# Turning attention probabilities with VectorE blocks and DMA in place of TensorE transposes

## The chip, the cores and the metric

The kernel runs on one core of one Trainium2 chip. Its time is the device time of one execution in microseconds; the median of the runs shown is what counts. Engines are named as in the profile: PE is TensorE (PEld its weight loads), DVE is VectorE, ACT is ScalarE, POOL is GpSimd, SP is SyncE, which issues the transfers.

## What is computed

Sparse attention, and then a gated MLP on its result:

```python
scores = q @ k.T / sqrt(64) - slope[h] * dist       # B=4, H=8, S=768, D=64
keep   = (key < 8) | ((0 <= q_pos - k_pos) & (q_pos - k_pos < 96))
a      = softmax(where(keep, scores, -1e9))
x      = (a @ v) laid out as [3072, 512]
out    = ((x @ w_a) * (x @ w_b)) @ w_out            # 512 -> 1536 -> 512, all float32
```

A block of 128 queries needs its own 128 keys, the 96 before them and 8 global ones: 232 columns, or 128 or 256 for the first two blocks of a batch.

## The kernel before

The 24 blocks of 128 queries (4 batches of 6) are cut into eight units of 4, 2, 3, 3, 3, 3, 3, 3 blocks. A unit's attention gives x for its 256 to 512 tokens, and its MoE (`moe`, L866) multiplies them by the weights, which are loaded once (`load_w`, L405, in units 0 and 1's time) and stay in SBUF. While PE does the MoE of unit u, the attention of unit u+1 goes on beside it. Float32 values are held as a high and a low part, and three products (high x high, low x high, high x low) give one exact enough product; this is why each MoE product shows three matmuls.

The MoE of a unit has 12 steps. A step makes two projections p of 12 matmuls each (L902) into two PSUM banks, p0 and p1, copies the first out (L387), multiplies it by the second (L941), makes the high and low part (hh at L387 or L389, hl at L397), and adds the product with w_out of the step before to acc (L920, 3 matmuls for each of the unit's blocks). After the twelfth step acc is copied out and stored (L973), three stores a unit.

The attention of units 2 to 7 (`attention`, L819) goes over four pairs of heads and, in each, over two heads and the unit's three blocks. For each head the raw q and k are loaded (`fetch`, L514, SP, two buffers) and split (`split`, L530); v is loaded once a pair (L522). For each block:

- scores into a bank psS (L844),
- softmax into a tile t of [128 queries, keys] (L583 DVE, L599 ACT, L614 and L621 DVE, normalisation at L631 ACT or L633 DVE), three buffers,
- `turn` (L648): a PE transpose for each chunk of 128 keys (L658) into a bank psT, and one copy to pf (L387 ACT or L389 DVE), so that the keys lie on partitions; pf has six buffers.

A block has one chunk when it is the first of its batch, otherwise two. After a pair's six blocks the values (`values`, L663) are multiplied: for every chunk and both heads a matmul with v as the stationary and pf as the moving operand (L675), 20 or 24 in a group, and the result is copied to x. Units 0 and 1 (`quad`, L687) do the same two heads at a time in another layout, also with `turn`.

No loop of the program sets the order. Every operation goes into a plan (`Schedule`) with a due time, an estimated cost for each engine that may do it, and the buffers that it reads and writes. The plan is played through once: each engine takes, in order of due time, the first operation that is ready and whose buffers are free; cheap choices (ACT or DVE for a copy) fall to whoever is free. The order found is written out as five fixed queues, which wait for each other by semaphores. A transfer counts in the plan as time on one engine "dma", and 2300 ns more until its data may be used. The operations of the first two units are tried in 400 random variants and the best kept. Attention is spread over 12 - SLACK steps of the unit before it:

```python
xs[u] = self.attention(u, t, t + (NF - SLACK) * steps[u - 1])
```

Of the kernel before, what the change touches and what calls it, by code (L numbers as in the profile page):

```python
# [13 lines left out]
F32 = mybir.dt.float32  # L14
F32R = mybir.dt.float32r
I32 = mybir.dt.int32
# [9 lines left out]
P = 128  # L26
# [8 lines left out]
PAIRED = 2  # L35
RAWS = 2
TBUFS = 3
PFBUFS = 6
MBUFS = 3

START = 52000
WLEAD = 6000
LOADLEAD = 8000
SPLITLEAD = 3000
SLACK = 1.5
BACKLOG = 1.0


# [112 lines left out]
        return self.tile[key]  # L161


class Op:
    def __init__(self, index, due, costs, emit, reads, writes, spare, port):
        self.index, self.due, self.costs, self.emit, self.spare = index, due, costs, emit, spare
# [28 lines left out]
class Schedule:  # L195
# [7 lines left out]
        self.tags = {}  # L203

    def buf(self, *args, **kw):
        b = Buf(*args, **kw)
        self.tags.setdefault(b.tag, []).append(b)
        return b

# [142 lines left out]
class Fast:  # L352
# [13 lines left out]
    def open(self):  # L366
# [2 lines left out]
        self.sp = ctx.enter_context(tc.tile_pool(name="s", bufs=1))  # L369
        self.ps = ctx.enter_context(tc.tile_pool(name="ps", bufs=1, space=PSUM))  # L370

    def sbuf(self, shape, dtype, tag, name, bufs=1):
        return self.plan.buf(self.sp, shape, dtype, tag, name, bufs=bufs)

# [30 lines left out]
    def load_w(self, f, due):  # L405


        nc, op = self.nc, self.plan.op
        for g in range(2):
            raw = self.plan.buf(self.wp, [P, 2 * WN], I32, f"w{f}_{g}", f"wr{f}_{g}")  # L410
            w = self.plan.buf(self.wp, [P, 2 * WN], F32R, f"w{f}_{g}", f"wt{f}_{g}")
            self.w[f, g] = w
            st = self.sbuf([P, WN], I32, "wm", f"wm{f}_{g}", MBUFS)
            words = lambda raw=raw: raw[:, :].rearrange("p (n two) -> p n two", two=2)
            low = lambda words=words: words()[:, :, 0]
            high = lambda words=words: words()[:, :, 1]
            mi = lambda st=st: st[:, :]
            m = lambda st=st: st[:, :].bitcast(F32)
            op(
                due,  # L420
                lambda e, f=f, g=g, raw=raw: nc.sync.dma_start(raw[:, :].bitcast(I64), self.wts[f, g]),
                writes=[(raw, "lo"), (raw, "hi")],
                dma=2184,
            )
            op(
                due,
                lambda e, m=m, high=high: nc.scalar.activation(m(), high().bitcast(F32), AF.Abs),  # L427
                [(raw, "hi")],
                [st],
                act=act(WN) + 72,  # L430
            )
            op(
                due,
                lambda e, m=m: nc.vector.tensor_scalar(
                    m(), m(), EMIN, EMAX, op0=ALU.max, op1=ALU.min
                ),
                [],
                [st],
                port=BOTH,
                dve=dve(WN, True),  # L440
            )
            op(
                due,
                lambda e, mi=mi: nc.vector.tensor_scalar(
                    mi(), mi(), 3, 0x3FFFFFFF, op0=ALU.logical_shift_left, op1=ALU.bitwise_and
                ),
                [],
                [st],
                port=BOTH,
                dve=dve(WN, True),  # L450
            )
            op(
                due,
                lambda e, mi=mi, high=high: nc.vector.scalar_tensor_tensor(
                    mi(), high(), -0x40000000, mi(), op0=ALU.bitwise_and, op1=ALU.bitwise_or
                ),
                [(raw, "hi")],
                [st],
                port=BOTH,
                dve=dve(WN),  # L460
            )
            op(
                due,
                lambda e, low=low: nc.scalar.activation(  # L464
                    low(), low().bitcast(U32), AF.Copy, scale=2.0**-29
                ),
                [],
                [(raw, "lo")],
                act=act(WN) + 72,
            )  # L470
            op(
                due,
                lambda e, mi=mi, low=low: nc.vector.tensor_tensor(mi(), mi(), low(), op=ALU.add),
                [(raw, "lo")],
                [st],
                port=BOTH,
                dve=dve(WN),
            )
            hi, lo = (lambda w=w: w[:, :WN]), (lambda w=w: w[:, WN:])
            self.copy(due, hi, m, WN, [st], [(w, "H")])  # L480
            self.sub(due, lo, m, hi, WN, [st, (w, "H")], [(w, "L")], shared=False)
# [91 lines left out]
            )  # L573
        return qh, ql, kk

    def softmax(self, h, due, wins, ps, t, sm):

        nc, op, n = self.nc, self.plan.op, len(wins)
        for j, (o, w) in enumerate(wins):
            neg = self.negd if w > P else self.negd0  # L580
            op(
                due,
                lambda e, j=j, o=o, w=w, neg=neg: nc.vector.tensor_tensor_reduce(  # L583
                    t[:, o : o + w],
                    ps[:, o : o + w],
                    neg[:, :w],
                    -(2.0 ** -(h + 1)),
                    3.0e38,
                    ALU.add,
                    ALU.min,  # L590
                    sm[:, j : j + 1],
                ),
                [ps, neg],
                [(t, j), (sm, j)],
                dve=dve(w) + 10,
            )
            op(
                due,
                lambda e, j=j, o=o, w=w: nc.scalar.activation(  # L599
                    t[:, o : o + w],  # L600
                    t[:, o : o + w],
                    AF.Exp,
                    bias=sm[:, j : j + 1],
                    scale=-1.0,
                    accum_out=sm[:, n + j : n + j + 1],
                ),
                [(sm, j)],
                [(t, j), (sm, n + j)],
                act=act(w) + 200,
            )  # L610
# [34 lines left out]
                act=act(w) + 100,  # L645
            )

    def turn(self, due, wins, t, pt, pf, spare=0.0):  # L648

        nc = self.nc  # L650
        starts = []
        for o, w in wins:
            starts += [o] if w == P else [o, o + w - P]
        n = len(starts) * P

        def emit(e):
            for c, o in enumerate(starts):
                nc.tensor.transpose(pt[:, c * P : c * P + P], t[:, o : o + P], self.ident)  # L658

        self.plan.op(due, emit, [t], [pt], pe=len(starts) * 112, spare=spare)  # L660
        self.copy(due, lambda: pf[:, :n], lambda: pt[:, :n], n, [pt], [pf], psum=True)

    def values(self, due, pl, blocks, v, probs, pa):  # L663


        nc = self.nc

        def emit(e):
            for i in blocks:
                slots = pl.vslot[i]  # L670
                for c, slot in enumerate(slots):
                    for s in range(2):
                        pf, o = probs[s, i]
                        v0 = (s * pl.nv + slot) * D
                        nc.tensor.matmul(  # L675
                            pa[D * s : D * s + D, i * P : i * P + P],
                            v[:, v0 : v0 + D],
                            pf[:, o + c * P : o + c * P + P],
                            start=c == 0,
                            stop=c == len(slots) - 1,  # L680
                        )

        reads = [v] + [probs[s, i][0] for s in range(2) for i in blocks]
        n = sum(len(pl.vslot[i]) for i in blocks)
        self.plan.op(due, emit, reads, [pa], pe=n * 218 + 290, spare=SPARE if pl.late else 0.0)

    def quad(self, u, c, j, due, raw, v, pa, homes):  # L687
# [44 lines left out]
        for s in range(2):  # L732
# [11 lines left out]
            self.turn(due, wins, t, pt, pf)  # L744
            o = 0
            for i in blocks:
                probs[s, i] = (pf, o)
                o += len(pl.vslot[i]) * P
        if pa is None:
            pa = self.bank("psS", f"pa{n}")  # L750
# [68 lines left out]
    def attention(self, u, start, end):  # L819
# [8 lines left out]
        for c in range(NCC):  # L828
            probs = {}
            v = self.fetch_v(u, c, start + (2 * c + 1) * step - LOADLEAD)  # L830
            for s in range(2):
                h = 2 * c + s
                due = start + h * step
# [2 lines left out]
                for i in range(pl.nb):  # L836
                    due = start + h * step + (i + 1) * step / pl.nb
                    k0, w = pl.kwin[i]
                    n = f"{u}_{h}_{i}"
                    ps = self.bank("psS", "ps" + n)  # L840

                    def scores(e, i=i, k0=k0, w=w, ps=ps, qh=qh, ql=ql, kk=kk):
                        for m, q in enumerate((qh, ql)):
# [6 lines left out]
                            )  # L850

                    op(due, scores, [qh, ql, kk], [ps], pe=2 * pe(w))
                    t = self.sbuf([P, 2 * P], F32, "t", "t" + n, TBUFS)
                    sm = self.sbuf([P, 8], F32, "sm", "sm" + n, 6)
                    self.softmax(h, due, [(0, w)], ps, t, sm)
                    pt = self.bank("psT", "pt" + n)
                    pf = self.sbuf([P, 2 * P], F32, "pf", "pf" + n, PFBUFS)
                    self.turn(due, [(0, w)], t, pt, pf, SPARE)
                    probs[s, i] = (pf, 0)
            due = start + (2 * c + 2) * step  # L860
            pa = self.bank("psA", f"pa{u}_{c}")
            self.values(due, pl, range(pl.nb), v, probs, pa)
            self.result(u, c, due, pa, x)
# [514 lines left out]
```

## Time and profile before

| what | us |
|---|---|
| median of 3 runs | 767.13 (767.0 to 768.37) |
| the profiled execution | 766.51 |
| its span in the trace | 764.7 |
| PE busy | 743.8 |
| ACT busy | 434.6 |
| DVE busy | 427.5 |
| POOL busy | 5.8 |

The span is the time between the first and the last recorded instruction; the profiled execution is 1.8 us longer than that. A share of busy time is an average over the stages. Matmuls are pipelined: a row with 0.39 us may start its successor after 0.23, so the pace is read from the starts. In rows of groups stand the line, the engine, the operation, what it writes and reads, the count, and then the busy time, the mean ns of one, and the idle time before them with what ended it.

### The profile page before, as it was taken

The numbers are of one execution on the slowest core, as the hardware profiler recorded it, in microseconds if no ns is written. First come the engines' busy times: TensorE is split into PE (matmuls) and PEld (weight loads), VectorE is DVE, ScalarE is ACT, GpSimd is POOL, SyncE is SP. The second block draws the span as 40 slices with busy tenths as digits, with TensorE's granted clock in tenths as the row PEclk, the third lists the DMA queues.
The fourth block names the chain that finished last, engine by engine and source line by source line (L and its number), as shares of the span: only waits on it lengthen the run. The fifth ranks groups of instructions, "written<-read, shape, count | busy, mean of one in ns | idle before, by whom it ended". The sixth has DMA issues, their size and how long they took to land.

```text
span 764.7 us, 12536 instructions
## 1 busy us (share of the span) xinstructions
PE 743.8 (97%) x4608; PEld 661.7 (87%) x4608; DVE 427.5 (56%) x1367; ACT 434.6 (57%) x1101; POOL 5.8 (1%) x25
## 2 busy tenths in 40 slices
PE   5789999999999999999999999999999999999996
PEld 4567778799999989999989999899989999989995
DVE  6999999755665555454445554444553645422111
ACT  7999756566665655555555655565554655441111
POOL 1000000000000000000000000000000000000000
PEclk9999999999999999999999999999999999999998
DMA  7896010132222111111212211111122111010001
GB/s 281 353 402 270 20 29 16 45 110 63 61 89 61 57 39 48 62 42 49 61 47 75 61 58 31 49 59 48 51 61 68 48 47 41 1 41 1 1 1 45
DMA packets 20085, 57.25 MB, mean 75 GB/s; under 512 B 2352, under 2 KB 2608, under 8 KB 20016
## 3 DMA queue, kind: packets, MB, share of 16 engines
q1 hardware_dynamic: 20016, 56.37, 22.2%
q8 instruction: 38, 0.62, 0.3%
q14 instruction: 31, 0.25, 0.1%
HBM read 50.07 MB, written 6.29 MB: 74 GB/s over the span
## 4 chain that ended last, share of the span: by engine, by line
PE 92%; ACT 4%; DVE 3%; issue 1%; DMA 0%; ACTq 0%
PE p L902 51%; PE acc L920 26%; PE pa L675 5%; PE pt L658 5%; PE ps L844 4%; PE ps L722 1%; ACT t L599 1%; DVE kk L397 1%; DVE t L583 1%; ACT wr L464 1%; ACT t L631 1%; ACT pf L387 1%; ACT wm L427 1%; DMA nv<-ns 0%; DVE ql L551 0%
## 5 line engine op out<-in xcount | busy, mean ns | idle before, releaser
L902 PE MATMUL p<-xh,wt 128*128 128x384 f32 (+2 forms) x1488 | 440.0, 344 | 0.6 <-ACT raw L387 0.5
L902 PEld LDWEIGHTS p<-xh,wt 128*128 128x128 f32 x1488 | 272.6, 188 | 14.4 <-issue 2.7
L902 PE MATMUL p<-xl,wt 128*128 128x384 f32 (+2 forms) x816 | 269.7, 341 | 1.2 <-ACT xl L387 0.9
L920 PE MATMUL acc<-wt,hh 128*128 128x512 f32 x576 | 208.1, 398 | 0.0
L902 PEld LDWEIGHTS p<-xl,wt 128*128 128x128 f32 x816 | 153.7, 189 | 10.5 <-ACT xl L387 1.2
L920 PEld LDWEIGHTS acc<-wt,hh 128*128 128x128 f32 x576 | 108.2, 188 | 19.5 <-issue 0.9
L599 ACT ACTIVATE t<-t,sm 128x232 f32<-128x232 f32 (+2 forms) x192 | 91.5, 479 | 44.7 <-DVE sm L583 42.4
L920 PE MATMUL acc<-wt,hl 128*128 128x512 f32 x288 | 113.1, 393 | 0.0
L583 DVE CUSTOM_DVE_ANT_0 t<-ps,rel 128x232 f32<-128x232 f32 (+1 forms) x160 | 63.1, 401 | 86.5 <-PE ps L844 84.7
L941 DVE TENSOR_TENSOR raw<-p,raw 128x384 f32<-128x384 f32 (+2 forms) x96 | 53.3, 555 | 100.7 <-PE p L902 85.0
L631 ACT ACTIVATE t<-t,sm 128x232 f32<-128x232 f32 (+2 forms) x129 | 61.7, 482 | 54.3 <-DVE sm L621 52.8
L387 ACT COPY raw<-p 128x384 f32<-128x384 f32 (+2 forms) x95 | 45.6, 480 | 82.0 <-PE p L902 81.9
L387 ACT COPY pf<-pt 128x256 f32<-128x256 f32 (+3 forms) x153 | 56.8, 376 | 24.9 <-PE pt L658 23.5
L658 PE MATMUL pt<-ident,t 128*128 128x128 f32 x352 | 67.3, 278 | 3.4 <-DVE t L633 2.0
L397 DVE TENSOR_TENSOR hl<-raw,hh 128x384 fp32r<-128x384 f32 (+2 forms) x96 | 53.3, 556 | 24.4 <-ACT hh L387 24.0
L387 ACT CAST hh<-raw 128x384 fp32r<-128x384 f32 (+2 forms) x91 | 46.5, 511 | 28.6 <-DVE raw L941 28.4
L658 PEld LDWEIGHTS pt<-ident,t 128*128 128x128 f32 x352 | 44.2, 140 | 19.4 <-ACT t L631 7.5
L920 PEld LDWEIGHTS acc<-wt,hl 128*128 128x128 f32 x288 | 54.3, 188 | 6.7
L614 DVE TENSOR_SCALAR sm<-sm 128x1 f32<-128x1 f32 (+1 forms) x168 | 25.7, 153 | 39.2 <-ACT t L599 37.5
L675 PE MATMUL pa<-pf,v 128*64 128x128 f32 x640 | 42.4, 278 | 3.0 <-DVE xl L781 2.5
L675 PEld LDWEIGHTS pa<-pf,v 128*64 128x64 f32 x640 | 34.5, 136 | 11.9 <-issue 4.6
L397 DVE TENSOR_TENSOR kk<-raw,kk 64x348 fp32r<-64x348 f32 (+1 forms) x92 | 42.7, 464 | 2.9
(79 smaller groups left out, 599.2 us busy)
## 6 DMA issues: line engine op xcount, KB each, us to landing
wr<-wts SPq DMA_DIRECT2D x24, 768.0 KB, 12.7
raw<-qkv SPq DMA_DIRECT2D x24, 366.0 KB, 3.0
raw<-qkv SPq DMA_DIRECT2D x24, 314.0 KB, 2.9
v<-qkv SPq DMA_DIRECT2D x16, 384.0 KB, 3.1
out<-o SPq DMA_DIRECT2D x23, 256.0 KB, 2.0
v<-qkv SPq DMA_DIRECT2D x16, 256.0 KB, 2.6
raw<-qkv SPq DMA_DIRECT2D x3, 616.0 KB, 6.2
raw<-qkv SPq DMA_DIRECT2D x5, 360.0 KB, 3.9
```

What stands on the lines that cost most here:

```text
L387: self.nc.scalar.copy(out(), src())
L397: lambda e: self.engine(e).tensor_sub(out(), a(), b()),
L583: lambda e, j=j, o=o, w=w, neg=neg: nc.vector.tensor_tensor_reduce(t[:, o : o + w], ps[:, o : o + w], neg[:, :w], -(2.0 ** -(h + 1)), 3.0e ...
L599: lambda e, j=j, o=o, w=w: nc.scalar.activation(t[:, o : o + w], t[:, o : o + w], AF.Exp, bias=sm[:, j : j + 1], scale=-1.0, accum_out=sm[ ...
L614: lambda e: nc.vector.tensor_scalar_add(sm[:, 2 * n : 3 * n], sm[:, n : 2 * n], 1e-9),
L631: nc.scalar.mul(t[:, o : o + w], t[:, o : o + w], r)
L658: nc.tensor.transpose(pt[:, c * P : c * P + P], t[:, o : o + P], self.ident)
L675: nc.tensor.matmul(pa[D * s : D * s + D, i * P : i * P + P], v[:, v0 : v0 + D], pf[:, o + c * P : o + c * P + P], start=c == 0, stop=c == ...
L844: nc.tensor.matmul(ps[:, :w], q[:, i * P : i * P + P], kk[:, k0 : k0 + w], start=m == 0, stop=m == 1,)
L902: nc.tensor.matmul(p[:, :T], wt(), b[:, b0 : b0 + T], start=c == 0 and n == 0, stop=c == NCC - 1 and n == 2,)
L920: nc.tensor.matmul(acc[i][:, :], hs[:, i * P : i * P + P], wt(), start=f == 0 and n == 0, stop=f == NF - 1 and n == 2,)
L941: lambda e, asb=asb, pb=pb: nc.vector.tensor_mul(asb[:, :T], pb[:, :T], asb[:, :T]),
```

## The change

In units 2 to 7 the PE transposes and the copies out of psT go. In their place `blocks32` (DVE) transposes a block's t in squares of 32x32, within each group of 32 partitions, into a buffer tp of 12 chunks for the whole pair of heads; then `swap` issues 16 transfers (SP), each from one group of 32 partitions of tp to one of pf, which carry the squares to the partitions of their keys. tp and pf are single buffers for a pair. The values read pf in four runs of 32 columns. tp, and three further buffers for t, lie in the scratch of the weight preparation (wm), which is idle by then; softmax in these units is made to wait for the last of it. The scores alternate between the banks psS and psT, and SLACK grows from 1.5 to 3. Units 0 and 1 keep `turn`.

```diff
-PFBUFS = 6
+CHUNKS = 12
+SQ = 32
-SLACK = 1.5
+SLACK = 3.0
...
+        self.wm = self.sbuf([P, MBUFS * WN], I32, "wm", "wm")
+        self.tp = self.plan.add(Over(self.wm, 0, CHUNKS * P, "tp"))
+        ats = range(CHUNKS * P, MBUFS * WN, 2 * P)
+        self.spares = [self.plan.add(Over(self.wm, at, 2 * P, f"t{at}")) for at in ats]
...
+    def blocks32(self, due, w, t, slot, n):
+        nc, tp = self.nc, self.tp
+        def emit(e):
+            src = t[:, :w]
+            dims = [[w - P, n]] * (n > 1) + [[SQ, P // SQ], [1, SQ]]
+            src = bass.AP(src.tensor, src.offset, [list(src.ap[0])] + dims)
+            dst = tp[:, :].rearrange("p (b m i) -> p m b i", b=P // SQ, m=CHUNKS)
+            dst = dst[:, slot : slot + n] if n > 1 else dst[:, slot]
+            nc.vector.transpose(dst, src)
+        done = [(self.wm, k) for k in range(MBUFS)]
+        self.plan.op(due, emit, [t] + done, [(tp, slot)], port=BOTH, dve=120 + 1.042 * n * P)
+
+    def swap(self, due, pf, m):
+        nc, tp, n = self.nc, self.tp, CHUNKS * SQ
+        for a in range(P // SQ):
+            for b in range(P // SQ):
+                out = lambda a=a, b=b: pf[SQ * b : SQ * b + SQ, a * n : a * n + m * SQ]
+                src = lambda a=a, b=b: tp[SQ * a : SQ * a + SQ, b * n : b * n + m * SQ]
+                self.plan.op(
+                    due,
+                    lambda e, out=out, src=src: nc.sync.dma_start(out(), src()),
+                    [tp],
+                    [(pf, (a, b))],
+                    dma=480,
+                )
...
             v = self.fetch_v(u, c, start + (2 * c + 1) * step - LOADLEAD)
+            pf = self.sbuf([P, CHUNKS * P], F32, "pf", f"pf{u}_{c}", 1)
+            slot = 0
...
-                    ps = self.bank("psS", "ps" + n)
+                    ps = self.bank(("psS", "psT")[(pl.nb * h + i) % 2], "ps" + n)
...
-                    t = self.sbuf([P, 2 * P], F32, "t", "t" + n, TBUFS)
+                    turn = (pl.nb * h + i) % (TBUFS + len(self.spares))
+                    if turn < TBUFS:
+                        t = self.sbuf([P, 2 * P], F32, "t", "t" + n, TBUFS)
+                    else:
+                        t = self.spares[turn - TBUFS]
...
-                    pt = self.bank("psT", "pt" + n)
-                    pf = self.sbuf([P, 2 * P], F32, "pf", "pf" + n, PFBUFS)
-                    self.turn(due, [(0, w)], t, pt, pf, SPARE)
-                    probs[s, i] = (pf, 0)
+                    chunks = len(pl.vslot[i])
+                    self.blocks32(due, w, t, slot, chunks)
+                    def get(k, slot=slot, pf=pf):
+                        view = pf[:, :].rearrange("p (a m i) -> p m a i", a=P // SQ, m=CHUNKS)
+                        return view[:, slot + k]
+                    probs[s, i] = (pf, get)
+                    slot += chunks
             due = start + (2 * c + 2) * step
+            self.swap(due, pf, slot)
```

More of the change, by code (lines that the diff above doesn't have):

```diff
@@ L161, in __getitem__, with __init__ @@
         return self.tile[key]
+class Over(Buf):
+    def __init__(self, home, at, cols, name):
+        super().__init__(None, None, F32, name, name)
+        self.home, self.at, self.cols = home, at, cols
+    def __getitem__(self, key):
+        if self.tile is None:
+            self.tile = self.home[:, self.at : self.at + self.cols].bitcast(F32)
+        return self.tile[key]
 class Op:
@@ L205, in buf, with add @@
     def buf(self, *args, **kw):
-        b = Buf(*args, **kw)
+        return self.add(Buf(*args, **kw))
+    def add(self, b):
         self.tags.setdefault(b.tag, []).append(b)
@@ L412, in load_w @@
             self.w[f, g] = w
-            st = self.sbuf([P, WN], I32, "wm", f"wm{f}_{g}", MBUFS)
+            ring = (2 * f + g) % MBUFS
+            st = (self.wm, ring)
+            m0 = ring * WN
             words = lambda raw=raw: raw[:, :].rearrange("p (n two) -> p n two", two=2)
@@ L416, in load_w @@
             high = lambda words=words: words()[:, :, 1]
-            mi = lambda st=st: st[:, :]
-            m = lambda st=st: st[:, :].bitcast(F32)
+            mi = lambda m0=m0: self.wm[:, m0 : m0 + WN]
+            m = lambda mi=mi: mi().bitcast(F32)
             op(
@@ L574, in split, with softmax @@
         return qh, ql, kk
-    def softmax(self, h, due, wins, ps, t, sm):
+    def softmax(self, h, due, wins, ps, t, sm, done=()):
         nc, op, n = self.nc, self.plan.op, len(wins)
@@ L592, in softmax @@
                 ),
-                [ps, neg],
+                [ps, neg, *done],
                 [(t, j), (sm, j)],
@@ L646, in softmax, with turn @@
             )
-    def turn(self, due, wins, t, pt, pf, spare=0.0):
+    def turn(self, due, wins, t, pt, pf):
         nc = self.nc
@@ L658, in emit @@
                 nc.tensor.transpose(pt[:, c * P : c * P + P], t[:, o : o + P], self.ident)
-        self.plan.op(due, emit, [t], [pt], pe=len(starts) * 112, spare=spare)
+        self.plan.op(due, emit, [t], [pt], pe=len(starts) * 112)
         self.copy(due, lambda: pf[:, :n], lambda: pt[:, :n], n, [pt], [pf], psum=True)
+    def blocks32(self, due, w, t, slot, n):
[22 more added lines that the diff above has]
+                )
     def values(self, due, pl, blocks, v, probs, pa):
@@ L672, in emit @@
                     for s in range(2):
-                        pf, o = probs[s, i]
                         v0 = (s * pl.nv + slot) * D
@@ L677, in emit @@
                             v[:, v0 : v0 + D],
-                            pf[:, o + c * P : o + c * P + P],
+                            probs[s, i][1](c),
                             start=c == 0,
@@ L746, in quad @@
             for i in blocks:
-                probs[s, i] = (pf, o)
+                get = lambda c, pf=pf, o=o: pf[:, o + c * P : o + c * P + P]
+                probs[s, i] = (pf, get)
                 o += len(pl.vslot[i]) * P
@@ L852, in attention @@
                     op(due, scores, [qh, ql, kk], [ps], pe=2 * pe(w))
-                    t = self.sbuf([P, 2 * P], F32, "t", "t" + n, TBUFS)
-                    sm = self.sbuf([P, 8], F32, "sm", "sm" + n, 6)
-                    self.softmax(h, due, [(0, w)], ps, t, sm)
-                    pt = self.bank("psT", "pt" + n)
-                    pf = self.sbuf([P, 2 * P], F32, "pf", "pf" + n, PFBUFS)
-                    self.turn(due, [(0, w)], t, pt, pf, SPARE)
-                    probs[s, i] = (pf, 0)
+                    turn = (pl.nb * h + i) % (TBUFS + len(self.spares))
[3 more added lines that the diff above has]
+                        t = self.spares[turn - TBUFS]
+                    sm = self.sbuf([P, 8], F32, "sm", "sm" + n, 6)
+                    self.softmax(h, due, [(0, w)], ps, t, sm, [(self.wm, k) for k in range(MBUFS)])
+                    chunks = len(pl.vslot[i])
[3 more added lines that the diff above has]
+                        return view[:, slot + k]
+                    probs[s, i] = (pf, get)
+                    slot += chunks
             due = start + (2 * c + 2) * step
+            self.swap(due, pf, slot)
             pa = self.bank("psA", f"pa{u}_{c}")
```

## The prediction

> **What bounds the kernel now.** I read the page first: busy time, the 40 slices, the chain that ended last.
>
> ```profile
> span 764.7 us, 12536 instructions
> PE 743.8 (97%) x4608; PEld 661.7 (87%) x4608; DVE 427.5 (56%) x1367; ACT 434.6 (57%) x1101; POOL 5.8 (1%) x25
> ...
> PE   5789999999999999999999999999999999999996
> ...
> PEclk9999999999999999999999999999999999999998
> ...
> PE 92%; ACT 4%; DVE 3%; issue 1%; DMA 0%; ACTq 0%
> PE p L902 51%; PE acc L920 26%; PE pa L675 5%; PE pt L658 5%; PE ps L844 4%; PE ps L722 1%; ACT t L599 1%; DVE kk L397 1%; DVE t L583 1%; ACT wr L464 1%; ACT t L631 1%; ACT pf L387 1%; ACT wm L427 1%; DMA nv<-ns 0%; DVE ql L551 0%
> ```
>
> From the fourth slice on TensorE (PE) never rests, at an undiminished clock, and it is 92% of the chain. A busy PE could still be one with stretched instructions, so I asked for stages, for the stores that mark their ends, and for the chain in order of time.
>
> ```profile
> 157.00:218.00 61.00, 61.00 (x483) 56.34 (x483) 40.29 (x167) 41.35 (x127) 0.00 (x0) 1.00 0.25 71
> 345.00:437.00 92.00, 91.93 (x570) 83.41 (x569) 46.45 (x164) 51.59 (x138) 0.71 (x1) 1.00 0.19 57
> ```
>
> ```profile
> 313.93 3.08 SPq L973 DMA_DIRECT2D out<-o  x3
> ```
>
> ```profile
> 683.58 76.40 SPq L973 DMA_DIRECT2D out<-o  x7
> ```
>
> ```profile
> 392.98 2.09 PE acc L920 x9
> 395.07 2.12 PE p L902 x12
> ```
>
> In the first fence the columns are stage, length, busy PE, PEld, DVE, ACT, POOL. A full stage is one unit's MoE beside the next unit's attention. Four of them lie between the stores at 313.93 and 683.58: 92.4 us each. The last unit has no attention beside it and takes 76.4. Its work is 12 steps of 24 p and 9 acc matmuls: 12 x (2 x 2.12 + 2.09) = 76. So attention costs a stage 16 us, which is nearly what its own matmuls take: PE is the bound, not one of its waits, and PE time taken out there should come off the end. DVE and ACT are at 50 to 56% in a full stage, at 66 to 68% in the short one (157 to 218, where unit 1 has two blocks).
>
> **What is removed.** Units 2 to 7 lose L658. Units of blocks 0, 1, 2 have 5 chunks a head, those of blocks 3, 4, 5 have 6: 3 x 40 + 3 x 48 = 264 transposes, the other 88 of 352 staying in units 0 and 1. A pipelined matmul's duration isn't its price; the step to the next start is.
>
> ```profile
> 446.61 0.39 PE L920 MATMUL acc<-wt,hl 128*128 128x512 f32 x1
> 446.83 0.40 PE L920 MATMUL acc<-wt,hh 128*128 128x512 f32 x1
> 447.07 0.38 PE L658 MATMUL pt<-ident,t 128*128 128x128 f32 x2
> 447.21 0.47 PE L920 MATMUL acc<-wt,hh 128*128 128x512 f32 x1
> 447.52 0.39 PE L920 MATMUL acc<-wt,hl 128*128 128x512 f32 x1
> 447.75 0.39 PE L920 MATMUL acc<-wt,hh 128*128 128x512 f32 x1
> ```
>
> An acc matmul takes 0.23 us from start to start (447.52 to 447.75). Two transposes and one acc take 447.52 - 447.07 = 0.45, so a transpose is 0.11, and the chain agrees (5% of 764.7 over 352 is 0.11). 264 x 0.112 = **29.6 us** off PE, 4.5 or 5.4 a stage, all in stages where PE is full. With rounding a transpose lies between 0.105 and 0.115: 27.7 to 30.4.
>
> The page "VectorE: DVE Perf Modes" of the Trainium skill, section "The three transpose paths", gives 390 ns for a 128x128 transpose (bf16) on TensorE and 311 on VectorE, and its rules prefer TensorE. By 390 ns the removal would be 103 us, more than 16 us of attention in a stage leave room for; the trace's 0.11 decides. An estimate from its 311 ns is 82 us more on DVE.
>
> ```profile
> L387 ACT COPY pf<-pt 128x256 f32<-128x256 f32 x119 | 44.0, 370 | 21.2 <-PE pt L658 20.7
> L387 ACT COPY pf<-pt 128x128 f32<-128x128 f32 x18 | 4.8, 265 | 3.5 <-PE pt L658 2.8
> L389 DVE COPY pf<-pt 128x128 f32<-128x128 f32 x6 | 1.8, 292 | 12.8 <-PE pt L658 12.8
> ...
> L397 DVE TENSOR_TENSOR hl<-raw,hh 128x256 fp32r<-128x256 f32 x12 | 5.1, 421 | 2.3 <-ACT hh L387 2.3
> ...
> L389 DVE CAST hh<-raw 128x256 fp32r<-128x256 f32 x2 | 0.6, 288 | 0.0
> ...
> L1241 DVE TENSOR_TENSOR rel<-rel,after 128x128 f32<-128x128 f32 x1 | 0.3, 294 | 0.0
> ```
>
> The 144 copies out of pt go too: 48.8 us of ACT, 2 of DVE. ACT is off the path; that buys nothing by itself, but the planner can move DVE's casts to it.
>
> **What is added on DVE.** 120 block transposes of two chunks, 24 of one. The trace shows none. Bounds for two chunks: 0.29 (a copy within SBUF, L389) and 0.59 (twice 0.294, each chunk with its own fixed part). I take the nearest rows, operations at one element a cycle: 0.42 and 0.29. A stage gets 8 x (0.29 + 2 x 0.42) = 9.1 or 8 x 3 x 0.42 = 10.1 us. In a full stage DVE goes from 46.5 to about 56 of 87 us: covered, cost 0. In the short one from 40.3 to 49.4 of 56.5, or 87%: little cover, so I charge 2 us there (0 to the stage's whole gain of 4.5).
>
> **What is added on the queues.** 24 pairs of heads x 16 transfers = 384, of 32 partitions x 1280 or 1536 B (at most 49 KB). Nothing of that size and direction is in the trace; the nearest are the first loads, issued one after the other, a run of weight loads, and the stores' landing.
>
> ```profile
> 6.02 0.33 SPq L510 DMA_DIRECT2D v<-qkv  x1
> ...
> 8.98 0.36 SPq L510 DMA_DIRECT2D v<-qkv  x1
> ...
> 43.91 11.71 SPq L421 DMA_DIRECT2D wr<-wts  x12
> ```
>
> ```profile
> DMA to landing us min/median/max: 2.0/2.1/4.1
> ```
>
> Seven issues in 8.98 - 6.02 = 2.96, six steps: 0.49 each. Where the queue waited for earlier loads it was 11.71 / 12 = 0.98. I take 0.48: the sixteenth is issued 7.2 us after the first and lands 2.1 later, 9.3 us in all; the other end is 0.98 x 15 + 2.1 = 16.8. SP's few loads and stores are issued far apart, so its queue has room: 384 x 0.48 = 184 of 540 us.
>
> Three waits are new. (1) SP: the first transfer waits for the pair's last turned block, and for the values of the pair before (one pf). Behind it stand later raw and v loads, ordered by due time. (2) DVE: the next pair's first block waits for all 16 landings (one tp). Behind it stand L941 and the hl subtraction, for which PE's p1 bank and back matmuls wait. Six t buffers (three in the idle weight scratch) let a whole pair's softmax run on meanwhile, and the planner counts 16 x 480 + 2300 ns = 10 us before it places that block, more than my 9.3. (3) PE: the values wait for 16 landings, and behind them stands everything. They can stand late in the order; the price I see is in the waiting itself.
>
> ```profile
> 284.74 0.40 PE L920 MATMUL acc<-wt,hh 128*128 128x512 f32 x1
> 285.06 1.53 PE L675 MATMUL pa<-pf,v 128*64 128x128 f32 x24
> 286.52 0.44 PE L658 MATMUL pt<-ident,t 128*128 128x128 f32 x2
> ```
>
> ```profile
> L844 PEldq EVENT_SEMAPHORE  x4: 51/51/51, 344.7 to 557.3; - x4
> ```
>
> Now a values group begins 285.06 - 284.74 - 0.23 = 0.09 late. A wait instruction on PE's queue takes 0.05; some eight more would be 0.41 if none is hidden by the matmuls in flight, 0 if all are. I take 0.1: 24 x 0.1 = 2.4 us (0 to 9.8). The values read pf in four strided runs of 32; I count that at 0, since their pace here is that of the rows streamed, with an upper end of the group's own 1.46 us again, 35 us, which I think far off.
>
> The scores now alternate between two banks, psT being free. The trace shows almost no PE idle time to win there: 0 to -1 us. A new order of the first two units (a random search) can differ by a us or two either way.
>
> **The sum**, against the profiled execution (766.5 us: a span of 764.7 and 1.8 around it): 766.5 - 29.6 + 2.0 + 2.4 = 741.3. The median shown, 767.1, is 0.6 above it: **742**, and 734 to 750 for this case.
>
> **Rivals.**
> *B, the first stage and the values eat half.* In the short stage four pairs have 56.5 us, 14 each, and each needs 9.3 for its transfers plus 6 x 0.42 = 2.5 for its blocks, with semaphores about 13; DVE is at 87%. For it: those numbers. Against: the order can begin earlier. Late by up to 10 us there, with the unhidden waits of 9.8 less the 4.4 already charged: 742 + 15 = 757.
>
> *C, nothing left.* The pair's longer chain (9.3 us where a copy of 0.37 stood) makes the next unit's inputs late at each of six stage ends by the 4.9 us won: 767. Against: a full stage gives a pair 21 us, and 13 are needed.
>
> *D, slower: DVE stands before a tp not yet free.* Mechanism (2) with transfers slower than planned. PE's work between two uses of p1 (12 p and 9 acc, 2.12 + 2.09) absorbs 4.2 us of it; the rest is paid 24 times. The gain is 29.6 / 24 = 1.2 us a pair, so it turns slower where the transfers take 10 + 4.2 + 1.2 = 15.4 us, an issue every 0.89. At 0.98 the last lands after 16.8: 24 x (16.8 - 14.2) = 62 us of loss, 766.5 - 29.6 + 62 = 799. For it: the weight loads did step at 0.98. Against: those are 768 KB each, sixteen times the size.
>
> *E, each transfer pays its whole latency.* 16 x 2.1 = 33.6 us a pair against 21 that it has: 24 x (33.6 + 2.5) = 866 us in place of 541 (157 to 698), or about 1090. Against: the first loads overlap, one each 0.49 us. The Trainium skill, "DMA: Bandwidth & Descriptors", section "Rules for kernel authors", says that transfers under 64 KB are mostly overhead and should be coalesced; by it this is the case that comes, but the trace's steps of 0.49 say that overhead here overlaps.
>
> That the change doesn't do what it says I give nothing: without L658 in those units, only the new way can fill pf.
>
> **How the numbers follow.** Forecast 0.52 (734 to 750), B 0.25 (750 to 764), C 0.05, D 0.16, E 0.02. About 0.2% (1.5 us) is what a measurement here can tell from no change. Faster: 0.52 + 0.25 = 0.77; same 0.05; slower 0.18. A range from 733 to 769 holds forecast, B and C, 0.82 less a little at its lower edge; D and E lie outside.
>
> **What would show it.** Right: L658 only in units 0 and 1, 88 times; stages near 87.5 us by the stores; PE full in them; DVE at some 65%; block transposes near 0.42; transfers about 0.48 apart. B shows as idle PE before L675, or as a first stage that isn't shorter than 61. D shows as DVE idle before the block transpose, released by a DMA, with PE idle before L902 behind it. E shows in the DMA steps alone. The prediction is wrong if block transposes cost over 0.6 us, if the step between transfers nears 0.9, or if values on strided pf take more than 1.46 us a group.

## The result and the profile after

The changed kernel takes 769.8 us against 767.2 before, a ratio of 1.0032 (95% interval 1.0019 to 1.0045): 0.3% slower, where 742 us had been forecast. The profiled execution took 769.24 us. Its page, the lines on PE's share and on the chain that ended last:

```profile
span 767.5 us, 12583 instructions
PE 719.2 (94%) x4344; PEld 643.1 (84%) x4344; DVE 456.4 (59%) x1476; ACT 398.8 (52%) x983; POOL 12.7 (2%) x34
...
PE   5799999999898999999989999999899999999996
...
PE 46%; SPq 26%; DVE 12%; DMA 6%; issue 5%; ACT 4%; DVEq 0%; ACTq 0%
SPq L713 26%; PE p L970 25%; PE acc L988 13%; DMA pf<-wm 6%; PE pa L730 4%; DVE wm L699 2%; DVE kk L420 2%; DVE ql L576 1%; PE ps L777 1%; DVE t L608 1%; PE ps L902 1%; DVE wm L608 1%; PE pt L683 1%; ACT t L624 1%; DVE kk L412 1%
```

Lines have moved: the values are L730, the projections L970, acc L988, `blocks32` L699, the transfers L713. PE did lose work (743.8 us busy became 719.2), but it is now idle for 48 us in place of 21 (the spans less these), and the row of slices has lost its unbroken nines. The chain, 92% PE before, now runs a quarter of its way through SP's queue, at the line that issues the transfers. (SPq is SP's queue. The issue of a transfer is the time that an engine's queue spends on starting it, its landing what follows until its data may be used.) Who made PE wait, from the view of waits (us in total, times, longest):

```profile
PE pa L730 <- DMA pf<-wm: 24.9, 21, 2.0
PE ps L777 <- DVE rel L1321: 5.8, 1, 5.8
PE pa L730 <- issue: 3.9, 3, 2.1
```

The middle row was there before (at L722). The other two are new, and they are the answer to where the gain went: all of the 24 groups of values wait, 21 for a transfer and 3 under "issue", where the profile names nobody: 24.9 + 3.9 = 28.8 us together, 1.2 each. One pair of heads in the chain in order of time, without its middle:

```profile
427.30 0.58 SPq L713
427.93 0.58 SPq L713
...
436.06 0.60 SPq L713
436.69 1.91 DMA pf<-wm
438.80 1.53 PE pa L730 x24
```

and the same place on PE's timeline:

```profile
436.77 0.34 PE L970 MATMUL p<-xh,wt 128*128 128x384 f32 x1
438.80 1.42 PE L730 MATMUL pa<-pf,v 128*64 128x128 f32 x22 [1.69 <-DMA pf<-wm]
```

The transfers are issued one after the other, a step of 427.93 - 427.30 = 0.63 us; the last lands at 438.6; PE's last projection matmul was over at 437.1, and its next instruction in order, the values, can start only at 438.8. The rows of the line L713 (min/median/max in ns, then the landing in us), and SP's timeline for this pair:

```profile
L713 SPq DMA_DIRECT2D pf<-wm x384: 507/589/2127, 167.4 to 675.7; - x192
...
DMA to landing us min/median/max: 1.8/1.9/4.6
```

```profile
426.73 10.55 SPq L713 DMA_DIRECT2D pf<-wm  x16
```

From the first issue to the last landing this is 438.6 - 426.7 = 11.9 us; the plan, by 16 x 480 + 2300 ns, reckoned with 10.0, and I with 9.3. The stages, by the stores at their ends:

```profile
319.59 3.78 SPq L1041 DMA_DIRECT2D out<-o  x3
```

```profile
686.75 76.24 SPq L1041 DMA_DIRECT2D out<-o  x7
```

Four full stages take (686.75 - 319.59) / 4 = 91.8 us, against 92.4 before: the transposes' 5 us are gone from each, and four waits of 1.2 us and more stand in their place.

VectorE did what was foreseen of it. Groups by shape: block transposes of two chunks from the spare t buffers and from the others, and of one chunk; and the transposes left to PE in units 0 and 1.

```profile
L699 DVE STREAM_TRANSPOSE wm<-wm 128x256 f32<-128x256 f32 x60 | 25.2, 430 | 8.5 <-ACT wm L656 8.3
...
L699 DVE STREAM_TRANSPOSE wm<-t 128x256 f32<-128x256 f32 x60 | 22.7, 417 | 23.8 <-DMA pf<-wm 22.2 <-ACT t L656 1.3 <-DMA out<-o 0.2
...
L683 PE MATMUL pt<-ident,t 128*128 128x128 f32 x88 | 14.5, 293 | 2.7 <-DVE sm L646 2.0 <-DVE t L658 0.3 <-ACT t L656 0.2
```

### The profile page after: what moved, and what is told of

Read it like the earlier page. It is cut to its first block, busy times and chain, and to the rows that moved or that the text cites. A ratio compares the mean times of both kernels' runs of the same rounds, so it can differ in the third digit from the quotient of the medians.

```text
span 767.5 us, 12583 instructions
## 1 busy us (share of the span) xinstructions
PE 719.2 (94%) x4344; PEld 643.1 (84%) x4344; DVE 456.4 (59%) x1476; ACT 398.8 (52%) x983; POOL 12.7 (2%) x34
## 4 chain that ended last, share of the span: by engine, by line
PE 46%; SPq 26%; DVE 12%; DMA 6%; issue 5%; ACT 4%; DVEq 0%; ACTq 0%
SPq L713 26%; PE p L970 25%; PE acc L988 13%; DMA pf<-wm 6%; PE pa L730 4%; DVE wm L699 2%; DVE kk L420 2%; DVE ql L576 1%; PE ps L777 1%; DVE t L608 1%; PE ps L902 1%; DVE wm L608 1%; PE pt L683 1%; ACT t L624 1%; DVE kk L412 1%
## 5 line engine op out<-in xcount | busy, mean ns | idle before, releaser
L970 PE MATMUL p<-xh,wt 128*128 128x384 f32 (+2 forms) x1488 | 419.1, 339 | 2.7 <-DVE wt L412 1.7
L970 PEld LDWEIGHTS p<-xh,wt 128*128 128x128 f32 x1488 | 271.1, 189 | 17.5 <-issue 3.0
L970 PE MATMUL p<-xl,wt 128*128 128x384 f32 (+2 forms) x816 | 270.5, 341 | 0.5 <-DVE xl L837 0.3
L988 PE MATMUL acc<-wt,hh 128*128 128x512 f32 x576 | 205.3, 397 | 0.0
L970 PEld LDWEIGHTS p<-xl,wt 128*128 128x128 f32 x816 | 153.7, 189 | 10.1 <-DVE xl L837 0.6
L988 PEld LDWEIGHTS acc<-wt,hh 128*128 128x128 f32 x576 | 108.8, 189 | 21.8 <-issue 2.1
L988 PE MATMUL acc<-wt,hl 128*128 128x512 f32 x288 | 113.6, 394 | 0.0
L410 ACT CAST hh<-raw 128x384 fp32r<-128x384 f32 (+2 forms) x87 | 44.1, 507 | 56.6 <-DVE raw L1009 55.9
L730 PE MATMUL pa<-pf,v 128*64 128x128 f32 x640 | 43.1, 278 | 30.8 <-DMA pf<-wm 24.9
L730 PEld LDWEIGHTS pa<-pf,v 128*64 128x64 f32 x640 | 35.8, 138 | 40.4 <-issue 33.0
L624 ACT ACTIVATE t<-t,sm 128x232 f32<-128x232 f32 (+2 forms) x120 | 57.1, 480 | 20.3 <-DVE sm L608 19.2
L988 PEld LDWEIGHTS acc<-wt,hl 128*128 128x128 f32 x288 | 54.5, 189 | 7.4
L608 DVE CUSTOM_DVE_ANT_0 t<-ps,rel 128x232 f32<-128x232 f32 (+1 forms) x100 | 39.0, 399 | 34.1 <-PE ps L902 32.3
L656 ACT ACTIVATE t<-t,sm 128x232 f32<-128x232 f32 (+2 forms) x86 | 40.4, 485 | 21.0 <-DVE sm L646 16.8
L699 DVE STREAM_TRANSPOSE wm<-t 128x256 f32<-128x256 f32 (+1 forms) x72 | 25.7, 399 | 42.4 <-DMA pf<-wm 39.8
L624 ACT ACTIVATE wm<-wm,sm 128x232 f32<-128x232 f32 (+2 forms) x72 | 34.2, 476 | 18.7 <-DVE sm L608 18.3
L656 ACT ACTIVATE wm<-wm,sm 128x232 f32<-128x232 f32 (+2 forms) x57 | 26.9, 477 | 28.7 <-DVE sm L646 21.1
L420 DVE TENSOR_TENSOR kk<-raw,kk 64x348 fp32r<-64x348 f32 (+1 forms) x82 | 38.5, 470 | 2.5
L902 PE MATMUL ps<-kk,ql 128*128 128x128 f32 (+1 forms) x144 | 39.4, 275 | 0.0
```

The source lines that it names most:

```text
L410: self.nc.scalar.copy(out(), src())
L420: lambda e: self.engine(e).tensor_sub(out(), a(), b()),
L624: lambda e, j=j, o=o, w=w: nc.scalar.activation(t[:, o : o + w], t[:, o : o + w], AF.Exp, bias=sm[:, j : j + 1], scale=-1.0, accum_out=sm[ ...
L656: nc.scalar.mul(t[:, o : o + w], t[:, o : o + w], r)
L699: nc.vector.transpose(dst, src)
L730: nc.tensor.matmul(pa[D * s : D * s + D, i * P : i * P + P], v[:, v0 : v0 + D], probs[s, i][1](c), start=c == 0, stop=c == len(slots) - 1,)
```

## The experiments

Two theories on the 28.8 us. **P (place)**: the values stand too early in PE's queue, because the plan believes that the data is there after 10 us; correct the belief or the transfers, and the gain appears. **L (loop)**: the loop of blocks, transfers and values over one tp and one pf is too long for a pair, and PE would wait wherever the values stand. A third, **R** (random draw), is on the first two units only: where unit 1 begins is a matter of the order that the random search happens to find. Each time stands beside runs of the kernel before on the same chip; the ratio is to those. The last column adds up what the values waited for a transfer or under "issue".

| run | edit | us | ratio to before (95%) | full stage, us | idle before values, units 2 to 7 |
|---|---|---|---|---|---|
| after | | 769.8 | 1.0032 (1.0019 to 1.0045) | 91.8 | 28.8 |
| e1 | plan 640 ns | 745.2 | 0.9695 (0.9679 to 0.9712) | 86.7 | none |
| e2 | plan 900 ns | 766.4 | 0.9978 (0.9963 to 0.9992) | 91.9 | 2.5 |
| e3 | values 2.6 us later | 751.8 | 0.9790 (0.9766 to 0.9814) | 88.1 | 5.0 |
| e4 | one transfer a pair | 736.2 | 0.9577 (0.9555 to 0.9599) | 86.9 | 1.3 |
| e5 | plan 560 ns | 744.1 | 0.9693 (0.9670 to 0.9716) | 87.7 | 3.1 |
| e6 | before, other draw | 769.7 | 1.0008 (0.9998 to 1.0018) | 92.4 | |
| e7 | plan 640 ns, other draw | 743.9 | 0.9670 (0.9653 to 0.9686) | 86.7 | none |
| e8 | plan 640 ns, SLACK 1.5 | 773.3 | 1.0057 (1.0040 to 1.0074) | 92.2 | 5.8 |
| e9 | half the transfers on POOL | 736.7 | 0.9594 (0.9577 to 0.9611) | 86.7 | none |
| e10 | half the transfers on ACT | 741.6 | 0.9665 (0.9644 to 0.9687) | 87.0 | 1.3 |
| e11 | plan 600 ns | 742.0 | 0.9666 (0.9648 to 0.9685) | 87.1 | 1.6 |
| e12 | as e9, SLACK 1.5 | 743.4 | 0.9673 (0.9657 to 0.9689) | 88.2 | none |

**e1: the plan told the truth.** In `swap`:

```diff
-                    dma=480,
+                    dma=640,
```

> The plan counts 640 ns in place of 480 for each of the 16 transfers; nothing else is edited. Theory P (place): the 28.8 us that TensorE idles before the values' matmuls are there because the plan puts the values where it expects the data, and a transfer takes 0.635 us and not 0.48; with the true price the idle time falls below 6 us and the kernel takes 741 to 750 us. Rival L (loop): the loop of blocks, transfers and values over one tp and one pf is too long whatever the plan believes, so the waits stay or move to the stage ends: 764 to 772 us.

It took 745.2 us. In the four stages between stores PE has no idle time left; from the view by stages (start and end, length, busy PE with its matmuls, PEld, DVE, ACT, POOL, clock, DMA share, GB/s), the first and the last of them:

```profile
312.58:398.89 86.31, 86.31 (x526) 80.05 (x525) 49.82 (x182) 44.54 (x118) 2.12 (x3) 1.00 0.31 88
...
572.38:659.47 87.09, 87.09 (x542) 80.81 (x541) 49.83 (x177) 44.02 (x113) 0.92 (x1) 1.00 0.26 74
```

The same work, the same transfers, one constant in the plan: some 25 us. L is refuted for the kernel as it stands. (A constant of the plan moves the order of everything else too; e9 below leaves the order as it is.)

**e2: the plan told too much.**

```diff
-                    dma=480,
+                    dma=900,
```

> The plan counts 900 ns for each transfer, more than it takes: 16.7 us for a pair in place of a true 12.4. Theory P: no idle time before the values (under 3 us), and as long as a pair's 21 us of a full stage hold it, 742 to 750 us; some 5 us more if the short first stage is too tight for it. Rival L: as long as with 480 or longer, 767 to 780 us.

It took 766.4, 16 us over the upper end of what P had said. The values don't wait (one of 2.5 us), but the stages are as long as before. PE's timeline at a stage end shows why:

```profile
320.03 1.53 PE L730 MATMUL pa<-pf,v 128*64 128x128 f32 x24
322.49 0.30 PE L902 MATMUL ps<-kk,qh 128*128 128x128 f32 x1 [0.93 <-DVE sm L608]
...
323.60 0.37 PE L902 MATMUL ps<-kk,qh 128*128 128x232 f32 x1 [0.38 <-DVE sm L639]
...
325.67 0.44 PE L902 MATMUL ps<-kk,qh 128*128 128x128 f32 x1 [1.59 <-ACT t L624]
...
326.55 0.52 PE L970 MATMUL p<-xl,wt 128*128 128x384 f32 x1
```

Over-caution pushed the pairs back until the last one's values (320.03) came when the MoE of the unit had nothing left: beside them only scores stand on PE, many of them waiting for softmax, until the next unit's projections go on at 326.13. These then run for a while at a slower pace (0.52 where 0.34 is usual). The stretch of 10 us from 320 (length, busy PE, granted clock, DMA share, GB/s):

```profile
320.00:330.00 10.00, 7.10 (x47) 0.76 0.44 127
```

From 220 to 690 the mean granted clock is 0.98, where it is 1.00 in e1. By an estimate from these two, 0.02 x 470 = 9 of the 21 us that e2 takes longer than e1 are this slower pace, and not the idle time itself. This is rival C of the prediction, and the grain of truth in L: the loop has no 5 us to give away in a stage.

**e3: only the values later.** In `values`:

```diff
-... pe=n * 218 + 290, spare=SPARE if pl.late else 0.0)
+... pe=n * 218 + 290, spare=2800.0 if pl.late else 0.0)
```

> The transfers are counted with 480 ns as in the changed kernel, so the block transposes keep their places in VectorE's queue; only the values are placed 2.6 us later in the plan (the extra lag before them is 2800 ns in place of 200). Theory P in the form that TensorE's own early place costs the time: idle before the values under 8 us, 744 to 753 us, with VectorE's 40 us of waiting for transfers still there. If VectorE's waiting before the block transposes is what counts: 760 to 768 us. Rival L: 764 to 772 us.

751.8 us. The waits of PE and of DVE for transfers:

```profile
PE pa L730 <- DMA pf<-wm: 3.3, 3, 1.6
```

```profile
DVE wm L699 <- DMA pf<-wm: 48.8, 18, 5.2
```

Here DVE stands before block transposes longer than in the changed kernel, whose row follows, and yet 18 us came back.

```profile
DVE wm L699 <- DMA pf<-wm: 39.8, 19, 5.7
```

It was PE's own place that cost most; DVE's standing may be part of the 7 us to e1, which no run separates.

**e4: one transfer.** The 16 operations of `swap` became one:

```diff
+        self.plan.op(due, lambda e: nc.sync.dma_start(pf[:, :], tp[:, :]), [tp], [pf], dma=2184)
```

> In place of the 16 transfers a pair has one, of all 128 partitions and 12 chunks (786 KB), counted in the plan with 2184 ns as a weight load is; this leaves out the exchange between the groups of 32 partitions, so the values are multiplied with wrongly placed probabilities. It keeps the block transposes, the lost TensorE transposes and all other edits. Theories P and L: the ceiling of the change, idle before the values under 5 us, 737 to 746 us. If something else of the change eats the gain (block transposes on VectorE, the values' strided reading, the other order of the first two units): 755 us or more.

736.2 us, just under the 737 to 746 expected: nothing else of the change eats the gain. The kernel leaves out the exchange between the groups of partitions, so its time is a bound and not a result. Its transfers, 768 KB each, land in 3.9 us, and an issue takes 0.47:

```profile
L709 SPq DMA_DIRECT2D pf<-wm x24: 464/471/529, 170.6 to 633.8; - x24
```

**e5 and e11: between.** The same constant at 560 and at 600.

> The plan counts 560 ns for each transfer, half-way between 480 and the 640 with which the waits went. Theory P: the idle time before the values lies between the 28.8 us of 480 and the none of 640, at 5 to 15 us, and so does the time, 747 to 758 us. If only the order that happens to come out counts and not the lateness of the data, the idle time follows no such line: as with 480 (over 22 us, 762 us or more) or as with 640.

> 600 ns in the plan, between 560 and 640, which took 744.1 and 745.2 us. Theory P: the data is about as early as planned; full stages of 86.7 us, and 738 to 747 us by what the first two units give.

744.1 and 742.0. With 560 the idle time before the values is 1.9 + 1.2 us, less than the 5 to 15 expected, and the time is as with 640, as the rival in this expectation had it: the lateness doesn't go over into waiting in proportion. An explanation that no run tests is that the values seldom stand at the very first moment that the plan allows. So these two runs don't separate the lateness of the data from the order that a price happens to give; e9 does.

```profile
PE pa L730 <- DMA pf<-wm: 1.9, 4, 0.7
...
PE pa L730 <- issue: 1.2, 3, 0.7
```

**e6 and e7: another draw of the search.** In the kernel before and in e1:

```diff
-        rnd = random.Random(1)
+        rnd = random.Random(2)
```

> The kernel before with another seed for the 400 random variants of the first two units; nothing else. Theory R: where unit 1's projections start (151.3 us before, 156.1 in the changed kernel, 158.4 with 640 ns, 152.6 with one transfer) is a matter of that draw and of the clock granted in the first 50 us, not of the transfers: it moves by some us here too, and the time with it, 764 to 772 us. Rival: the spread belongs to the change, and this kernel stays within 1 us of 767.

> The changed kernel with 640 ns in the plan and the other seed. Theory R: the full stages take the same 86.7 us, and the whole differs from the 745.2 of the first draw by what the first two units give: 737 to 750 us. Rival: the late start of 5 to 7 us belongs to the change and comes again: 744 to 747.

769.7 beside 769.1, and 743.9 beside e1's 745.2: a microsecond either way. The full stages are equal to 0.1 us. Unit 1's projections began at 153.3 in e6 and 157.3 in e7, against 151.3 and 158.4 with the first draw. So the draw moves the start by one or two us, and most of what the start is late with 640 ns stayed (7.1 us with the first draw, 4.0 with the second): R holds only in small, and its rival was closer.

**e8: the later due time.** On top of e1:

```diff
-SLACK = 3.0
+SLACK = 1.5
```

> The changed kernel with 640 ns in the plan and SLACK at 1.5 as before, so that the attention is due 1.5 steps later in each stage. If the pairs' longer chain needs the earlier due time, TensorE idles at the stage ends as it did with 900 ns: 752 to 768 us. If not, SLACK has no part in it: 742 to 748 us.

773.3: slower than before, with the picture of e2 (PE waits 8.5 us for DVE before scores and 5.8 before the values, and from 220 to 690 the mean granted clock is again below 1.00, at 0.97). SLACK is no decoration: a pair whose chain is some 10 us longer must be due earlier.

**e9: the transfers brought to the plan.** The plan stays at 480:

```diff
-                    lambda e, out=out, src=src: nc.sync.dma_start(out(), src()),
+                    lambda e, out=out, src=src, q=(nc.sync, nc.gpsimd)[b % 2]: q.dma_start(out(), src()),
```

> The changed kernel with its plan untouched (480 ns), but every second transfer issued from GpSimd's queue, which is nearly idle. It turns theory P round: not the plan is brought to the transfers, but the transfers to the plan. If eight issues on SP (8 x 0.635 = 5.1 us) and eight on POOL run side by side and land some 2 us later, the data is there after 7 to 9 us, before the plan's 10: idle before the values under 5 us, 740 to 748 us. If a POOL issue takes over 1.2 us, the data is as late as before or later: 765 us or more. Rival L: no change, 764 to 772.

736.7 us, below the 740 to 748 expected and 4.1% under the kernel before, the fastest of the kernels here that compute the whole of the reference. This is the cleanest of the comparisons: the matmuls of PE and the operations of DVE and ACT are one for one, in the same order, those of the changed kernel (4344, 1476 and 983 of them in both traces), so that another order has no part in the 33 us. Two of them stand before the first of these transfers (unit 1's projections begin at 154.1 in place of 156.1, the transfers at 165.3); the other 31 come from the way the transfers are issued. The two queues in its trace, ns for one:

```profile
L713 SPq DMA_DIRECT2D pf<-wm x192: 507/589/1880, 165.3 to 637.4; - x192
L713 POOL DMA_DIRECT2D pf<-wm x192: 496/496/682, 165.6 to 637.2; - x192
```

Eight issues take 5 us on SP and 4 on POOL, side by side, where sixteen took ten, and the values follow their predecessor with a gap of 0.09 us, as before the change (418.93 - 418.67 - 0.17):

```profile
418.67 0.34 PE L970 MATMUL p<-xh,wt 128*128 128x384 f32 x1
418.93 1.53 PE L730 MATMUL pa<-pf,v 128*64 128x128 f32 x24
420.39 0.44 PE L970 MATMUL p<-xh,wt 128*128 128x384 f32 x1
```

The same 92 us of the changed kernel and of e9, by the view by stages:

```profile
402.00:494.00 92.00, 86.19 (x530) 79.86 (x530) 53.28 (x184) 46.10 (x118) 0.70 (x1) 1.00 0.32 90
```

```profile
402.00:494.00 92.00, 92.00 (x570) 85.65 (x569) 56.65 (x197) 47.08 (x123) 17.10 (x34) 1.00 0.32 90
```

PE idle for 5.8 us in the first, for none in the second, which gets 40 matmuls further.

The Trainium skill, "DMA: Bandwidth & Descriptors", section "Issuing engines are not separate DMA queues", says that issuing from several engines saves only the sequencer's time, usually small beside the transfer. The traces agree that this alone is saved (a landing even takes 2.3 us in e9, by the median, and 1.9 in the changed kernel), but here it isn't small: 16 issues of 0.63 us stand beside a landing of 1.9.

**e10: the same with ACT.** `nc.scalar` in place of `nc.gpsimd`.

> The same with ScalarE's queue for every second transfer. Theory P: the data is early, but ScalarE spends eight issues of about 0.6 us a pair that the plan does not know of, 24 x 8 x 0.6 = 115 us on an engine 52% busy, in front of copies that TensorE's banks wait for: idle before the values gone, idle elsewhere in its place, 745 to 765 us.

741.6 us, a little better than expected: ACT spends 0.52 us on each of its 192 issues, but PE waits for copies of the MoE only once and 1.1 us longer than in e9 (acc for hh). Of the 4.9 us to e9 3.9 are there by the stores of the first short stage (225.17 against 221.27).

**e12: e9 with SLACK 1.5.**

> Half the transfers on GpSimd's queue as in the run that took 736.7 us, the plan at 480 ns, but SLACK at 1.5. With 640 ns in the plan, one queue and SLACK 1.5 the kernel took 773: TensorE idled at the stage ends, where the last pair's values come and nothing else is left to do. If that is due to the pair's chain alone, the shorter chain (7 us in place of 12) mends most of it: 737 to 748 us. If it is due to the late due time of the attention itself, whatever the chain: 758 to 775 us.

743.4 us, where e8 took 773: with the short chain the late due time costs 7 us and not 28. The two runs differ in the plan's price too (480 and 640), so this isn't a test of the chain alone.

## Why the prediction was wrong

Right: what bounds the kernel, and roughly the price of what goes. A full stage falls from 92.4 to 86.7 us in e1, e7 and e9, by 5.7 where 4.5 to 5.4 were reckoned; over 44 transposes a stage this is up to 0.13 us each in place of 0.112. The block transposes took 0.42 to 0.43 us (0.42 forecast), VectorE was covered, and busy for less than forecast (50 to 53 us in each of e9's four full stages, 56 of 87 forecast), the strided pf costs nothing (a group of 24 takes 420.39 - 418.93 = 1.46 as before), and the small transfers overlap (against rival E). Had the data been there in time, 742 would have been near: e11 took 742.0 and e9 went below. That e11 meets the forecast to the microsecond is luck: its full stages gained more than reckoned (5.3 us, against 4.9 on average), and its unit 1 begins later (155.9, against 151.3 before). The short first stage (rival B) has room after all: in e9 PE is busy for 62.7 of the 63 us from 157 to 220.

Wrong is the step on the third new wait: "They can stand late in the order; the price I see is in the waiting itself", at 0.1 us a group. They could stand late, but the plan puts them where it expects the data, and it has no reserve. The waits measured are 1.2 us a group, 28.8 in all, 26.4 more than the 2.4 charged. That step rested on another: the step of 0.48 us between issues, taken from loads out of HBM, where transfers from SBUF to SBUF of 32 partitions take 0.63, and so 11.9 us a pair in place of 9.3. It lay inside the bounds that I gave (up to 16.8); but I let lateness cost something only from 14.2 us on (and the kernel turn slower from 15.4), because I had it reach PE through DVE alone (rival D), where 4.2 us of PE's work absorb it. The direct way has no such cushion: with a plan of 10.0 us and transfers of 11.9, 1.9 us of lateness cost 1.2 us a group, and with a plan of 16 x 560 + 2300 ns = 11.3 (e5) they were 0.1. So the loss begins between 10 and 11.9 us and not at 14.2. Of rival D's sign one half came, DVE's idle time before the block transposes (39.8 us); the other half, idle PE before the projections behind it, did not:

```profile
L970 PE MATMUL p<-xh,wt 128*128 128x384 f32 (+2 forms) x1488 | 419.1, 339 | 2.7 <-DVE wt L412 1.7
```

Idle PE before the values, which did come, had been named as the sign of B, with other causes (unhidden wait instructions, a late first stage).

PE's busy time fell by 743.8 - 719.2 = 24.6 us and not by 29.6. The mean granted clock was 0.990 in the changed kernel and 0.997 before, and work at a slower pace counts as busy for longer: by an estimate from these, 0.007 x 767 = 5 us. Such a stretch is shown in the last section.

Part of the loss is also in the first two units: unit 1's projections begin at 156.1 in the changed kernel, 151.3 before. There the granted clock was 0.80 to 0.86 in three stretches of 10 us before 50, where it was 1.00 before. E9, in the same order, dips too (0.67 from 30 to 40) and begins unit 1 at 154.1. How much of the late start is the order and how much the clock stays open.

## What to carry to other kernels

When work is replaced by something with a longer latency, and the queues are written out from a plan, the plan's price for the new step is part of the change: too low, and a consumer stands in its queue before its data; too high, and the work comes too late at the stage's end. Here 480, 600 and 900 ns for the same transfer made 769.8, 742.0 and 766.4 us. Take such a price from the nearest transfer of the same kind (both ends, partitions), and ask of each new wait first what stands behind it on the engine that is the bound. Where the issuing of a burst of small transfers makes the latency, as here, a second queue shortens it.

## What the runs showed of the hardware

The issue time goes by the kind of transfer more than by its size. On SP a load from HBM mostly took 0.33 us, 128 partitions from SBUF to SBUF 0.47 (768 KB), 32 partitions 0.59 whether of 40 or of 48 KB. Why fewer partitions take longer was not tried.

A short idle time can cost twice. PE's timeline of the changed kernel, around its longest wait for values:

```profile
240.75 0.33 PE L970 MATMUL p<-xh,wt 128*128 128x384 f32 x1
243.18 1.94 PE L730 MATMUL pa<-pf,v 128*64 128x128 f32 x24 [2.10 <-issue]
...
245.64 0.63 PE L988 MATMUL acc<-wt,hl 128*128 128x512 f32 x1
246.07 1.05 PE L988 MATMUL acc<-wt,hh 128*128 128x512 f32 x2
...
248.14 0.40 PE L988 MATMUL acc<-wt,hh 128*128 128x512 f32 x1
248.38 0.34 PE L970 MATMUL p<-xh,wt 128*128 128x384 f32 x1
```

After 2.1 us without work the matmuls step at 246.07 - 245.64 = 0.43 us, where 248.38 - 248.14 = 0.24 is usual; the granted clock of that stretch of 10 us is 0.83, and 0.50 from 245 to 247. A wait almost as long left the pace as it was, in the stretch of 10 us from 550, whose clock is 1.00:

```profile
551.75 1.31 PE L730 MATMUL pa<-pf,v 128*64 128x128 f32 x20 [2.01 <-DMA pf<-wm]
553.00 0.50 PE L988 MATMUL acc<-wt,hh 128*128 128x512 f32 x1
553.34 0.40 PE L988 MATMUL acc<-wt,hl 128*128 128x512 f32 x1
...
554.03 0.39 PE L988 MATMUL acc<-wt,hl 128*128 128x512 f32 x1
554.26 0.39 PE L988 MATMUL acc<-wt,hh 128*128 128x512 f32 x1
```

The Trainium skill, "TensorE: Matmul & The Clock Gate", section "Part 1: The HAM clock gate", has the array at half pace after an idle window of about 3.4 us. The half pace agrees. The idle time was shorter here, 2.1 us, while 2.0 brought no drop. These two alone would allow a limit between them; but in e2 the clock fell to 0.50 (from 326 to 332) after single waits of 0.93, 0.38 and 1.59 us within some 4 us, as the timeline of e2 above shows. So the length of the last wait alone doesn't decide it; what does was not tried.
